# Four edits to the opening of a fused attention and double-MLP kernel: an early table load, two vectors on another queue, an earlier second pair, and square roots on another engine

## The chip, the cores and the metric

The kernel runs on one core of a Trainium2 chip. Its time is the device time of one execution in microseconds, and a kernel is judged by the median of several executions. One of them was taken with the hardware profiler; its trace and page are what is read below.

## The reference

`q`, `k` and `v` are [4, 12, 448, 64] in f32 (four batches, twelve heads, 448 rows, 64 columns). Everything that is computed:

```python
q_n = q / sqrt(mean(q*q, -1) + 1e-6) * g_q          # and k_n alike with g_k
attn = softmax(q_n @ k_n.T / 8)                      # per head
x = (attn @ v) laid out as [1792, 768]
h = x @ moe_w_in;   g = h * sigmoid(1.702 * h);   y = g @ moe_w_out       # 768 -> 2048 -> 768
h2 = y @ moe2_w_in; g2 = max(h2,0) + alpha*min(h2,0);  out = g2 @ moe2_w_out
```

Weights are f32 in memory. The two vectors g_q and g_k have 64 numbers each.

## The kernel before, in words

**Tiling and stages.** The twelve heads of a batch are handled as six pairs, so there are 24 pairs P (four batches b of six). A pair's q and k lie in one tile `qk` [128, 2, 7, 64], and its v in a second tile. `load_qk(P)` (L378 to L381) issues four transfers: the main rows of k and of q (192 KB each) and the remaining rows of k and of q (32 KB each). `load_v(P)` (L394 to L397) issues three. For the first batch both go to the queue of the sync engine SP, which issues them one after the other.

**The first batch** runs in f32. `normalize(P)` squares the pair on ScalarE in two halves (L421), sums each half on VectorE (L423) and computes the reciprocal roots of the 14 sums of every partition by a seed and three Newton steps (L424 to L434, 14 instructions on 128x14 elements; for a call with two pairs, 128x28), before the change always on GpSimd. `prep_pair(P)` multiplies q and k by the roots into `qn` (VectorE, L458), transposes `qn` on TensorE (L465, L467) and copies the result to SBUF on ScalarE (L468), k with the scale `g_col`, which holds the product of the gains. It then takes the maximum of v on VectorE (L470). The scores of the pair follow (L516, maximum L530, exponential L550).

**The gains.** `gains()` loads g_q and g_k, spread over the 128 partitions, multiplies them on VectorE (L284) and forms from them the scaled vector `gs` (L293), the constant `c_s` and, by a transposition on TensorE, the column `g_col` (L297).

**Weights beside it.** While the first pairs run, `weights(...)` streams the first layer's input weights through a ring of five raw buffers (transfers of 512 KB, L223, on SP's queue), turns each into f32 words (ScalarE L148, VectorE L164 and L165), takes row maxima (L245) and splits them into two f16 parts (L179, L180). The output weights follow. Then come the other three batches in f16 parts beside the first layer's products (L758, L798, L821), and at last the second layer (L927, L1090).

**The order of the work.** The program is written as generators that are advanced by hand (`first_pairs`, `attention`, `weights`), but the order in which an engine's instructions are issued is set by a planner, which moves ready work ahead of what is written before it, by priorities and a model of the times. On each engine's queue, and on SP's and GpSimd's transfer queues, work then runs in that fixed order. The opening is written in L1182 to L1191: identity and ones, `load_qk(0)`, `gains()`, `load_v(0)`, `load_qk(1)`, `load_v(1)`, then the first weight transfers, `normalize(0)`, `prep_pair(0)`, the loads of pair 2 and so on, and `normalize(1)`.

Of the kernel before, what the change touches and what calls it, by code (L numbers as in the profile page):

```python
# [9 lines left out]
F32 = mybir.dt.float32  # L10
# [47 lines left out]
def attention_moe_kernel(  # L58
# [220 lines left out]
    def gains():  # L279
        gq = small.tile([128, D], F32, tag="gq", name="gq", bufs=1)  # L280
        gk = small.tile([128, D], F32, tag="gk", name="gk", bufs=1)
        nc.sync.dma_start(out=gq, in_=g_q.partition_broadcast(128))
        nc.sync.dma_start(out=gk, in_=g_k.partition_broadcast(128))
        nc.vector.tensor_tensor(out=gq, in0=gq, in1=gk, op=ALU.mult)  # L284
        gm = small.tile([128, 1], F32, tag="gm", name="gm", bufs=1)
        gi = small.tile([128, 1], F32, tag="gi", name="gi", bufs=1)
        nc.vector.tensor_reduce(out=gm, in_=gq, op=ALU.max, axis=AX, apply_absolute_value=True)
        pow2floor(c_s, gm)
        scaled_reciprocal(gi, c_s, 0.5)
        nc.vector.memset(gs[64:128, 3], 1.0)  # L290
        for c in range(4):
            ps = slice(0, 64 if c == 3 else 128)
            nc.vector.tensor_scalar(out=gs[ps, c], in0=gq[ps], scalar1=gi[ps], scalar2=None, op0=ALU.mult)  # L293
        nc.vector.tensor_scalar(out=c_s, in0=c_s, scalar1=2.0 ** -22, scalar2=None, op0=ALU.mult)
        gt = ps_m.tile([128, 128], F32, tag="m", name="gt")
        nc.tensor.transpose(out=gt, in_=gs[:, 0:2].rearrange("p c d -> p (c d)"), identity=identf)
        nc.scalar.activation(out=g_col, in_=gt[:, 0:1], func=AF.Copy, scale=c_s)  # L297
# [111 lines left out]
    def normalize(*Ps):  # L409

        Ps = [P for P in Ps if P < B * NP]
        if not Ps:
            return
        n = NT2
        w = 2 * n * len(Ps)
        ss = small.tile([128, 4 * NT2], F32, tag="ss", name="ss")[:, 0:w]
        for t, P in enumerate(Ps):
            flat = raws[P].rearrange("p h c d -> p (h c) d")
            for i in range(2):
                sq = att_p.tile([128, n, D], F32, tag="sq", name="sq", bufs=SQB)  # L420
                nc.scalar.activation(out=sq, in_=flat[:, i * n:(i + 1) * n], func=AF.Square, scale=2.0 ** -13)  # L421
                o = (2 * t + i) * n
                nc.vector.tensor_reduce(out=ss[:, o:o + n], in_=sq, op=ALU.add, axis=AX)  # L423
        nc.gpsimd.tensor_scalar(out=ss, in0=ss, scalar1=1e-6 * 2.0 ** -20, scalar2=None, op0=ALU.add)  # L424
        rs = small.tile([128, 4 * NT2], F32, tag="rs", name="rs")[:, 0:w]
        tn = small.tile([128, 4 * NT2], F32, tag="tn", name="tn")[:, 0:w]
        nc.gpsimd.tensor_scalar(
            out=rs.bitcast(I32), in0=ss.bitcast(I32), scalar1=-0.5, scalar2=RSQRT_SEED, op0=ALU.mult, op1=ALU.add
        )
        for _ in range(3):  # L430
            nc.gpsimd.tensor_tensor(out=tn, in0=rs, in1=rs, op=ALU.mult)
            nc.gpsimd.tensor_tensor(out=tn, in0=tn, in1=ss, op=ALU.mult)
            nc.gpsimd.tensor_scalar(out=tn, in0=tn, scalar1=-0.5, scalar2=1.5, op0=ALU.mult, op1=ALU.add)
            rooted[Ps[0]] = nc.gpsimd.tensor_tensor(out=rs, in0=tn, in1=rs, op=ALU.mult)  # L434
        for t, P in enumerate(Ps):
            eng = side(P)
            ks = raws[P][:, :, 0:4]
            flat = raws[P].rearrange("p h c d -> p (h c) d")
            root = rs[:, 2 * n * t:2 * n * (t + 1)]
            if P < NP:  # L440
                roots[P] = root
                continue
            eng.tensor_tensor(out=ks, in0=ks, in1=gs.unsqueeze(1).to_broadcast([128, 2, 4, D]), op=ALU.mult)
            eng.tensor_tensor(out=flat, in0=flat, in1=root.unsqueeze(2).to_broadcast([128, 2 * n, D]), op=ALU.mult)
# [737 lines left out]
    if True:  # L1182
        make_identity(nc, ident)
        nc.vector.memset(ones, 1.0)
        nc.vector.tensor_copy(out=identf, in_=ident)
        load_qk(0)
        gains()
        load_v(0)
        load_qk(1)
        load_v(1)  # L1190
        g0 = big.tile([128, KF, 2, S], F16, tag="g", name="g0")  # L1191
        stage = g0.rearrange("p m e t -> p (m e t)").bitcast(F32)
        parts = stage[:, 0:R1I * 1024].bitcast(I32).rearrange("p (i n t) -> p i n t", i=R1I, t=2)
        raw1o = g0.rearrange("p m e t -> p m (e t)").bitcast(I32)[:, KF - 4 * R1O:, FIRST:].rearrange("p m (n t) -> p m n t", t=2)

        def num1i(j):
            if j == KD - 1:
                return stage[:, 5120:5120 + FF]
            return held.bitcast(F32)[:, (j - 3) * FF:(j - 2) * FF]

        def num1o(j):
            if j == KF - 2:
                return att_p.tile([128, 2 * NT2 * D], F32, tag="ph", name="num1o", bufs=PHB)[:, 0:DM]
            return raw_p.tile([128, 2 * NT2 * D], F32, tag="qk", name="num1o", bufs=QKB)[:, 0:DM]

        w1i_steps = weights(
            moe_w_in, "w1i", lambda: w1i, later_rows(w1i, 3, num1i), lambda t: parts[:, t % R1I], 4, R1I, 2.0 ** -14, scales,
            G1I
        )
        w1o_steps = weights(  # L1210
            moe_w_out, "w1o", lambda: w1o, later_rows(w1o, 2, num1o), lambda t: raw1o[:, 4 * (t % R1O):4 * (t % R1O) + 4], 2,
            R1O, 2.0 ** -25, scales, G1O
        )
        next(w1i_steps)
        normalize(0)
        for _ in prep_pair(0):
            pass
        for P in range(2, 1 + QKB):
            load_qk(P)
        load_v(2)  # L1220
        normalize(1)
        early = measure(1, B - 1, 4)
        for i, _ in enumerate(first_pairs()):
            if i >= 6:
                for _ in range(1):
                    next(early, None)
            for _ in range(W_RATE):
                next(w1i_steps, None)
        for _ in w1i_steps:
            pass  # L1230
        v_scales(0, v0)
        first_x()
        moe1_scales(0)
        for P in range(NP, NP + 2):
            load_qk(P)
            load_v(P)
        n1o = 0
        steps = attention([4 * P + r for P in range(NP) for r in range(2, 4)])
        for i, _ in enumerate(steps):
            pairs = max(0, (i - LAG + 1) // 2)  # L1240
            rows = KF - 2 if pairs >= 4 else (HOLD + pairs * HELD) // (2 * DM) - 2
            while n1o < min(1 + 2 * rows + 3 * (rows // 2), (i + 1) * W1O_RATE, 57):
                next(w1o_steps)
                n1o += 1
            if i >= M_AT and i - M_AT < KF:
                first_in(slice(0, FIRST), i - M_AT, g0)
            for _ in range(2):
                next(early, None)
        while n1o < 57:
            next(w1o_steps)  # L1250
            n1o += 1
        for m in range(len(range(2 * NP + LAG)) - M_AT, KF):
            first_in(slice(0, FIRST), m, g0)
        with tc.issue_after(loads["w1o"][W1O_HOLD].ins):
            normalize(NP, NP + 1)
            for _ in prep_pair(NP):
                pass
            load_qk(NP + 2)
            load_qk(NP + 3)
            load_v(NP + 2)  # L1260
        att_steps = other_batches()
        done = 4 * NP
        late = late_weights(ctx, att)
        for b in range(B):
            last = min(NU, 4 * NP * (b + 2)) + LAG2
            first = done
            got = None
            for i, _ in enumerate(moe1(b) if b else first_moe1(g0)):
                lead = 0 if b else B1_AT
                want = first + (last - first) * min(1.0, max(0.0, i + 1 - lead) / (PACE[b] * TICKS - lead))  # L1270
                while done < min(want, NU + LAG2):
                    next(att_steps)
                    done += 1
                if b == B - 1:
                    for _ in range(1 if i < 2 * KF else 2):
                        if got is None or i >= 2 * KF:
                            got = next(late, None)
        second_layer(late)
# [30 lines left out]
```

## Time and profile before

| what | value |
|---|---|
| time, median of 3 runs | 1150.96 us (1147.56 to 1157.47) |
| time of the profiled execution | 1150.36 us |
| its span, first to last instruction | 1148.6 us |
| TensorE (PE) busy | 1069.4 us, 93% of the span |
| VectorE (DVE) busy | 802.1 us, 70% |
| ScalarE (ACT) busy | 693.2 us, 60% |
| GpSimd (POOL) busy | 179.4 us, 16% |
| mean granted TensorE clock | 0.977 of full |
| moved by DMA | 158.19 MB, mean 138 GB/s |

The span is 1.8 us shorter than the execution's own time; what lies around it is not in the trace. Busy shares are averages over stages that differ: TensorE's 93% comes from the later stages, and the opening, where the diff is, looks different. Views by stretch and by order of time are therefore needed beside the table. "PEld" is TensorE's weight load, "SPq" the sync engine's queue of transfers.

### The profile page before, as it was taken

The numbers are of one execution on the slowest core, as the hardware profiler recorded it, in microseconds if no ns is written. First come the engines' busy times: TensorE is split into PE (matmuls) and PEld (weight loads), VectorE is DVE, ScalarE is ACT, GpSimd is POOL, SyncE is SP. The second block draws the span as 40 slices with busy tenths as digits, with TensorE's granted clock in tenths as the row PEclk, the third lists the DMA queues.
The fourth block names the chain that finished last, engine by engine and source line by source line (L and its number), as shares of the span: only waits on it lengthen the run. The fifth ranks groups of instructions, "written<-read, shape, count | busy, mean of one in ns | idle before, by whom it ended". The sixth has DMA issues, their size and how long they took to land.

```text
span 1148.6 us, 18408 instructions
## 1 busy us (share of the span) xinstructions
PE 1069.4 (93%) x6753; PEld 585.0 (51%) x6753; DVE 802.1 (70%) x1397; ACT 693.2 (60%) x1452; POOL 179.4 (16%) x364
## 2 busy tenths in 40 slices
PE   4776889898989999999999999999999999999998
PEld 2343457744444445555455455444444477666664
DVE  5979798887879885577534865599976224959341
ACT  4778686888879876688633562356456425756120
POOL 2701003676433342100000000000000000000000
PEclk9978899899999999999999999999999999999999
DMA  7974743478888756455446501765351423363111
GB/s 227 258 178 132 182 129 109 97 158 184 183 191 167 160 130 151 109 121 118 78 124 229 203 1 64 249 215 194 136 171 59 138 70 113 106 184 101 33 31 28
DMA packets 235562, 158.19 MB, mean 138 GB/s; under 512 B 167888, under 2 KB 214736, under 8 KB 235472
## 3 DMA queue, kind: packets, MB, share of 16 engines
q1 hardware_dynamic: 229200, 141.34, 44.6%
q0 software_dynamic: 6272, 15.67, 5.3%
q8 instruction: 53, 0.87, 0.3%
q14 instruction: 37, 0.30, 0.1%
HBM read 92.35 MB, written 25.69 MB: 103 GB/s over the span
## 4 chain that ended last, share of the span: by engine, by line
PE 56%; DVE 16%; DMA 11%; issue 7%; ACT 6%; POOL 4%; SPq 1%; DVEq 0%; POOLq 0%; ACTq 0%
PE op L1090 17%; PE yp L821 15%; PE h L927 9%; PE hp L798 7%; PE xp L648 3%; PE sp L525 2%; DMA t<-hl 2%; PE hp L758 2%; DMA g<-in_moe_w_in_dram 2%; DVE nm L530 1%; DMA g<-in_moe_w_out_dram 1%; DVE g L141 1%; ACT pr L550 1%; DMA qk<-in_q_dram 1%; DMA yr<-y_dram 1%
## 5 line engine op out<-in xcount | busy, mean ns | idle before, releaser
L821 PE MATMUL yp<-g,w1o 128*128 128x448 f16 x1152 | 226.9, 354 | 1.5 <-DVE g L767 0.9
L927 PE MATMUL h<-x,w2i 128*128 128x512 f16 (+1 forms) x1152 | 219.3, 352 | 4.3 <-DVE pos L933 2.8
L798 PE MATMUL hp<-x,w1i 128*128 128x448 f16 x864 | 170.3, 353 | 1.6 <-DVE t L807 1.6
L927 PEld LDWEIGHTS <-w2i 128*128 128x128 f16 x1152 | 112.6, 98 | 109.6 <-issue 5.1
L821 PEld LDWEIGHTS <-w1o 128*128 128x128 f16 x1152 | 109.5, 98 | 110.8 <-issue 12.0
L798 PEld LDWEIGHTS <-w1i 128*128 128x128 f16 x864 | 81.9, 98 | 83.5 <-issue 9.6
L620 DVE SCALAR_TENSOR_TENSOR ph<-pr,sm,ph 128x448 f16<-128x448 f32 x126 | 85.2, 707 | 25.4 <-ACT ph L593 25.4
L530 DVE TENSOR_REDUCE nm<-sp 128x2 f32<-128x896 f32 x96 | 92.5, 964 | 10.3 <-PE sp L525 7.6
L932 ACT ACTIVATE pos<-h,sign 128x512 f32<-128x512 f32 (+1 forms) x64 | 40.1, 628 | 89.7 <-PE h L927 83.3
L550 ACT ACTIVATE pr<-sp,nm,c_s 128x448 f32<-128x448 f32 x126 | 89.9, 717 | 2.4 <-DVE ph L620 1.1
L1090 PEld LDWEIGHTS <-even 128*128 128x128 f16 x672 | 65.7, 98 | 43.5
L933 DVE SCALAR_TENSOR_TENSOR pos<-h,slope,pos 128x512 f32<-128x512 f32 (+1 forms) x64 | 43.4, 680 | 59.9 <-ACT pos L932 59.7
L593 ACT ACTIVATE ph<-pr,sm 128x448 f16<-128x448 f32 x126 | 77.6, 659 | 10.7 <-DVE sm L590 10.6
L758 PE MATMUL hp<-x,w1i 128*128 128x256 f16 (+1 forms) x576 | 66.1, 276 | 9.2 <-DVE g L767 5.2
L1090 PEld LDWEIGHTS <-odd 128*128 128x128 f16 x504 | 49.3, 98 | 32.6
L758 PEld LDWEIGHTS <-w1i 128*128 128x128 f16 x576 | 55.2, 104 | 20.2 <-issue 14.8
L1090 PE MATMUL op<-w2lo,even 128*128 128x384 f16 x384 | 63.5, 326 | 0.0
L648 PE MATMUL xp<-pt,vs 128*64 128x256 f16 (+1 forms) x792 | 49.8, 267 | 7.5 <-DMA pt<-ph 6.2
L525 PE MATMUL sp<-t 64*128 64x448 f16 (+1 forms) x432 | 54.0, 357 | 0.6 <-DMA t<-hl 0.5
L648 PEld LDWEIGHTS <-vs 128*64 128x64 f16 x792 | 37.9, 112 | 27.6 <-issue 17.2
L532 ACT ACTIVATE nm<-nm,c_s 128x2 f32<-128x2 f32 x72 | 20.9, 290 | 48.5 <-DVE nm L530 48.1
L1090 PE MATMUL op<-w2hi,even 128*128 128x384 f16 x288 | 47.5, 326 | 0.0
(243 smaller groups left out, 1659.7 us busy)
## 6 DMA issues: line engine op xcount, KB each, us to landing
g<-in_moe_w_in_dram SPq DMA_DIRECT2D x24, 512.0 KB, 6.1
g<-in_moe_w_out_dram SPq DMA_DIRECT2D x32, 384.0 KB, 4.0
w2raw<-in_moe_w_in_dram SPq DMA_DIRECT2D x24, 512.0 KB, 5.7
w2raw<-in_moe_w_out_dram SPq DMA_DIRECT2D x16, 768.0 KB, 6.4
g_dram<-pos SPq DMA_DIRECT2D x48, 256.0 KB, 2.0
gp<-g_dram SPq DMA_DIRECT2D x8, 1024.0 KB, 6.8
odd<-g_dram SPq DMA_DIRECT2D x6, 1024.0 KB, 5.5
y_dram<-y SPq DMA_DIRECT2D x24, 224.0 KB, 2.5
```

What stands on the lines that cost most here:

```text
L525: nc.tensor.matmul(out=sp[:, j, 0:S] if n == 2 else sp[ds, 0, 0:S], lhsT=qt[ds] if n == 2 else qt[ds, 64:128], rhs=kt[ds, 0:S], start=(i = ...
L530: nc.vector.tensor_reduce(out=nm[:, 0:n], in_=sp[:, 0:n, 0:S], op=ALU.max, axis=AX, negate=True)
L550: last = nc.scalar.activation(out=pr[i], in_=sp[:, i, 0:S], func=AF.Exp, bias=nm[:, i:i + 1], scale=c_s if u >= 4 * NP else 1.0, accum_out ...
L593: nc.scalar.activation(out=ph[:, i, 0:S], in_=pr[i], func=AF.Copy, scale=sm[:, i:i + 1])
L620: nc.vector.scalar_tensor_tensor(out=ph[:, i, S:2 * S], in0=pr[i], scalar=sm[:, i:i + 1], in1=ph[:, i, 0:S], op0=ALU.mult, op1=ALU.subtract)
L648: nc.tensor.matmul(out=xp[64 * j:64 * j + 64, t:t + n], lhsT=vs[ks, j, c], rhs=pt[ks, 7 * j + kc, 0:n] if b else pt[ks, kc, o:o + n], star ...
L758: nc.tensor.matmul(out=ps, lhsT=w1i[:, kk, e, m * 128:(m + 1) * 128], rhs=xs[0, kk][:, f, cols], start=(i == 0), stop=(i == 3 * KD - 1))
L798: nc.tensor.matmul(out=ps, lhsT=w1i[:, kk, e, m * 128:(m + 1) * 128], rhs=x[:, f], start=(n == 0), stop=(n == 3 * KD - 1))
L821: nc.tensor.matmul(out=ps, lhsT=w1o[:, m, e, j * 128:(j + 1) * 128], rhs=g[:, m, f], start=(n == 0), stop=(n == 3 * KF - 1))
L927: nc.tensor.matmul(out=ps, lhsT=w2i[:, kk, e, m * 128:(m + 1) * 128], rhs=x2[kk][:, f], start=(c == 0), stop=(c == 3 * KD - 1))
L933: nc.vector.scalar_tensor_tensor(out=pos, in0=ps, scalar=slope[:, m:m + 1], in1=pos, op0=ALU.mult, op1=ALU.max)
L1090: nc.tensor.matmul(out=ps, lhsT=ops[:, o, m, f], rhs=rhs[:, e], start=(c == 0), stop=(c == 3 * KH - 1))
```

## The change

Four edits, all in the opening:

1. A small activation (`first`, 128x1, function Square, read from `ones`) is added ahead of everything else on ScalarE.
2. The transfers of g_q and g_k are issued by GpSimd instead of SP.
3. `load_qk(1)` is issued right after `load_qk(0)`, ahead of `load_v(0)`.
4. The 14 root instructions of pair 0 go to VectorE; those of all other pairs stay on GpSimd.

```diff
     def gains():
...
-        nc.sync.dma_start(out=gq, in_=g_q.partition_broadcast(128))
-        nc.sync.dma_start(out=gk, in_=g_k.partition_broadcast(128))
+        nc.gpsimd.dma_start(out=gq, in_=g_q.partition_broadcast(128))
+        nc.gpsimd.dma_start(out=gk, in_=g_k.partition_broadcast(128))
...
     def normalize(*Ps):
...
-        nc.gpsimd.tensor_scalar(out=ss, in0=ss, scalar1=1e-6 * 2.0 ** -20, scalar2=None, op0=ALU.add)
+        eng = nc.vector if Ps[0] < 1 else nc.gpsimd
+        eng.tensor_scalar(out=ss, in0=ss, scalar1=1e-6 * 2.0 ** -20, scalar2=None, op0=ALU.add)
...
-        nc.gpsimd.tensor_scalar(
+        eng.tensor_scalar(
             out=rs.bitcast(I32), in0=ss.bitcast(I32), scalar1=-0.5, scalar2=RSQRT_SEED, op0=ALU.mult, op1=ALU.add
         )
         for _ in range(3):
-            nc.gpsimd.tensor_tensor(out=tn, in0=rs, in1=rs, op=ALU.mult)
-            nc.gpsimd.tensor_tensor(out=tn, in0=tn, in1=ss, op=ALU.mult)
-            nc.gpsimd.tensor_scalar(out=tn, in0=tn, scalar1=-0.5, scalar2=1.5, op0=ALU.mult, op1=ALU.add)
-            rooted[Ps[0]] = nc.gpsimd.tensor_tensor(out=rs, in0=tn, in1=rs, op=ALU.mult)
+            eng.tensor_tensor(out=tn, in0=rs, in1=rs, op=ALU.mult)
+            eng.tensor_tensor(out=tn, in0=tn, in1=ss, op=ALU.mult)
+            eng.tensor_scalar(out=tn, in0=tn, scalar1=-0.5, scalar2=1.5, op0=ALU.mult, op1=ALU.add)
+            rooted[Ps[0]] = eng.tensor_tensor(out=rs, in0=tn, in1=rs, op=ALU.mult)
...
         make_identity(nc, ident)
         nc.vector.memset(ones, 1.0)
+        first = small.tile([128, 1], F32, tag="first", name="first", bufs=1)
+        nc.scalar.activation(out=first, in_=ones[:, 0:1], func=AF.Square)
         nc.vector.tensor_copy(out=identf, in_=ident)
         load_qk(0)
+        load_qk(1)
         gains()
         load_v(0)
-        load_qk(1)
         load_v(1)
```

## Rows read from the trace of the kernel before

**Rows 1.** Busy time by stretch; columns: engines, granted clock, DMA share, GB/s.
```profile
0.00:20.00 20.00, 5.10 (x15) 2.72 (x17) 8.97 (x25) 6.93 (x12) 7.44 (x33) 1.00 0.67 214
20.00:40.00 20.00, 11.87 (x37) 5.23 (x34) 19.50 (x32) 14.74 (x30) 8.88 (x24) 1.00 0.95 282
40.00:60.00 20.00, 15.86 (x102) 9.04 (x102) 18.36 (x37) 12.95 (x30) 14.61 (x37) 1.00 0.86 248
60.00:80.00 20.00, 17.44 (x80) 9.16 (x80) 16.55 (x32) 16.24 (x38) 1.68 (x3) 0.70 0.80 171
...
140.00:160.00 20.00, 18.54 (x132) 11.17 (x129) 15.69 (x39) 14.17 (x33) 0.00 (x0) 0.92 0.54 156
...
240.00:260.00 20.00, 20.00 (x160) 10.28 (x155) 16.93 (x29) 17.59 (x42) 15.86 (x25) 1.00 0.80 172
...
500.00:600.00 100.00, 100.00 (x685) 50.76 (x683) 59.58 (x101) 66.83 (x155) 3.84 (x6) 1.00 0.47 107
```

**Rows 2.** Order of time, the first pair's path from its load to `qn` on all engines.
```profile
2.55 0.61 SPq L381 DMA_DIRECT2D qk<-in_q_dram  x1
...
4.79 1.28 ACT L421 ACT_TABLE_LOAD   x1 [4.79 <-DMA qk<-in_q_dram]
...
6.09 1.04 ACT L421 ACTIVATE sq<-qk 128x448 f32<-128x448 f32 x2
...
8.60 0.23 DVE L284 TENSOR_TENSOR gq<-gq,gk 128x64 f32<-128x64 f32 x1 [1.28 <-DMA gk<-in_g_k_dram]
8.74 0.61 DVE L423 TENSOR_REDUCE ss<-sq 128x7 f32<-128x448 f32 x1
...
9.45 0.26 POOL L424 TENSOR_SCALAR ss<-ss 128x14 f32<-128x14 f32 x1 [8.15 <-DVE ss L423]
...
13.34 0.22 POOL L434 TENSOR_TENSOR rs<-tn,rs 128x14 f32<-128x14 f32 x1
13.59 1.09 DVE L458 TENSOR_TENSOR qn<-qk,rs 128x896 f32<-128x896 f32 x1 [0.39 <-POOL rs L434]
...
15.30 0.26 POOL L424 TENSOR_SCALAR ss<-ss 128x14 f32<-128x14 f32 x1 [1.74 <-DVE ss L423]
...
20.47 1.09 DVE L458 TENSOR_TENSOR qn<-qk,rs 128x896 f32<-128x896 f32 x1 [1.00 <-POOL rs L434]
```

**Rows 3.** Order of time, SP's queue from g_q to the first weights.
```profile
3.21 0.59 SPq L282 DMA_DIRECT2D gq<-in_g_q_dram  x1
...
4.32 0.43 SPq L394 DMA_DIRECT2D w1o<-in_v_dram  x1
...
6.10 0.59 SPq L378 DMA_DIRECT2D qk<-in_k_dram  x1
...
8.55 0.59 SPq L394 DMA_DIRECT2D w1o<-in_v_dram  x1
...
10.59 2.57 SPq L223 DMA_DIRECT2D g<-in_moe_w_in_dram  x5
```

**Rows 4.** Chain that ended last; start, length, what.
```profile
3.84 4.65 DMA gk<-in_g_k_dram
...
25.36 6.55 DMA qk<-in_q_dram
```

**Rows 5.** Order of time, short VectorE instructions of the gains, and v's maximum.
```profile
9.52 0.15 DVE L105 TENSOR_SCALAR c_s<-gm 128x1 f32<-128x1 f32 x1
9.70 0.15 DVE L106 TENSOR_SCALAR c_s<-c_s 128x1 int32<-128x1 int32 x1
...
10.00 0.69 DVE L470 TENSOR_REDUCE v<-w1o 128x1 f32<-128x512 f32 x1
```

**Rows 6.** Order of time, two transfers issued by GpSimd.
```profile
48.86 1.34 POOL L312 DMA_DIRECT2D vst<-in_v_dram  x2
```

**Rows 7.** Transfers by line; count, KB each, median us from issue to landing.
```profile
vr<-in_v_dram POOLq DMA_DIRECT2D x32, 32.0 KB, 3.1
```

**Rows 8.** Order of time: a load of the second layer, issued in the opening.
```profile
44.51 0.42 SPq L857 DMA_DIRECT2D slope<-in_moe_alpha_dram  x1
```

## The prediction

> **What bounds the kernel now.** I first read the busy time by stretch [rows 1], because the whole-span shares of 93% for TensorE and 70% for VectorE hide the order of the limits. From about 240 us on TensorE is busy nearly all the time; the stretches from 240 to 260 us (20.00 of 20) and from 500 to 600 us (100.00 of 100) stand for it. What starts there earlier ends earlier, so a microsecond saved in front reaches the end if it reaches 240 us. In front of that no engine is full all the time. In the first 20 us VectorE works 8.97 us and stands for 11.0, while the transfers are at a share of 0.67. From 20 to 40 us VectorE is busy 19.50 of 20 and the transfers are at 0.95: both are nearly full there, and the share of the transfers falls only after 40 us.
>
> Second, I read the opening in order of time [rows 2]. Pair 0's last load is issued at 2.55 us and releases ScalarE at 4.79, but ScalarE then loads its table of functions for 1.28 us, and the squares start at 6.09. The second sum's input is there at 7.13 (6.09 + 1.04), yet VectorE's queue holds the product of the gains in front of it, which waits 1.28 us for g_k; so the sum starts at 8.74. GpSimd's 14 instructions run from 9.45 to 13.56, and `qn` starts at 13.59. For pair 1 GpSimd starts at 15.30 and `qn` at 20.47, after VectorE stood still for 1.00 us.
>
> Third, SP's queue [rows 3]: g_q at 3.21, the first v at 4.32, pair 1's q and k at 6.10, the second v at 8.55, the first weights at 10.59. The chain that ended last [rows 4] runs through g_k (4.65 us from issue to landing), and at 25.36 through a load of q of 6.55 us. So the opening is a chain of latencies, and the 30 us behind it are bound by transfers as much as by VectorE.
>
> **The change part by part.** *Early table load.* The load needs nothing but ScalarE, which is idle before 4.79. Released by `ones`, ready about 1 us into the span, it and the small activation are over before pair 0 lands, and the squares start at 4.8 instead of 6.09: 1.3 us less on the path [rows 2]. The cover is the load of q and k. The Trainium skill, "ScalarE: Activation LUTs", section "What ACT_TABLE_LOAD costs", adds a drain of 1.38 us and so puts a switch at 2.66 us. This trace shows the 1283 ns but no drain behind them: the load ends at 6.07 and the squares begin at 6.09. By the page the term would be 2.7 us; I keep 1.3.
>
> *Gains on GpSimd's queue.* Two transfers leave SP: 4.32 − 3.21 = 1.11 us, by which everything after `load_v(1)`, the weights first, is issued earlier [rows 3]. GpSimd spends 1.34 us on two issues [rows 6] and is otherwise idle there until the sums come. It can issue them from about 1.3 us; they land 3.1 us later by the nearest row of its queue [rows 7], or at most 4.65 by the g_k of SP [rows 4]: at 5.1 to 7.3 us instead of 8.49. If the product of the gains still stands between the two sums, it costs VectorE at best no wait, and at worst, with squares ready at 5.86, about a microsecond; I take none. So the second sum ends near 6.7 instead of 9.36, of which 1.3 us is the table and 1.3 the gains.
>
> *Pair 0's roots on VectorE.* GpSimd takes 4.1 us (9.45 to 13.56). Dependent short instructions on VectorE follow each other every 0.18 us (9.52, 9.70 [rows 5]), on one element; the upper end is the product of the gains with 64 elements, 0.23 [rows 2], some 0.26 with the gap. So 14 of them cost 2.5 to 3.6 us; 14 elements are nearest the short rows, and I take 2.5. That is 1.6 us less in latency and 2.5 us more work for VectorE, which stands idle for 11.0 us of these 20 [rows 1]; without that cover it would cost its 2.5 us in full. If the gains' eleven instructions (2.2 us by rows like these) come ahead of the roots on VectorE's queue, `qn` is that much later. Together pair 0's `qn` starts at 9.2 to 11.4 instead of 13.59: 2.2 to 4.4 us earlier.
>
> *Pair 1 ahead of v.* Its four transfers take 2.45 us on SP (6.10 to 8.55) and move up by 2.89: 1.11 for the gains and 1.78 for the three transfers of v that they pass. GpSimd, free of pair 0, can start pair 1's roots near 10 instead of 15.30. The first v is issued 2.45 − 1.11 = 1.34 us later; the second v and the weights still gain 1.11. VectorE reads the first v at 10.00 [rows 5]; that cover is thin, which is a rival below.
>
> **The sum.** The latency chain gets 2.2 to 4.4 us shorter, the transfers start 1.11 us earlier. Between 15 and 40 us both limit, so I expect the front to move by something between 1.1 and 4.4 and take 2.5: 1150.36 − 2.5 = 1147.9 us, **1148**. The profiled execution lies 0.6 us under the median of the runs shown, well inside their spread of 10 us, so I make no correction.
>
> **Rivals.** *Only the transfers count.* With their share at 0.95 [rows 1] and a 6.55 us load on the chain [rows 4], an earlier `qn` only waits longer for weights; the result is 1.1 us or nothing, 1149.3 to 1150.4. For it: the full transfers. Against: the share is not 1.00, and the weights' ring is refilled only when VectorE has consumed it. The same time follows if the edits are inert, for instance if the planner places the table load or the gains so that nothing starts earlier. The Trainium skill, "DMA: Bandwidth & Descriptors", section "Issuing engines are not separate DMA queues", says that issuing from several engines saves only issue time; the trace agrees in that SP's issues, not the bytes of g_q and g_k (64 KB), are what stands ahead of the weights.
>
> *VectorE waits for the first v.* Now issued at 5.66 to 7.4, it lands by 11.5 at the latest (an issue at 6.8 plus 4.65 [rows 4]). If the maximum of v stays ahead of the roots in VectorE's order, they begin at 11.5 + 0.69 = 12.2 and `qn` at 14.7, 1.1 us later than before: 1151.5. It decides if v's maximum is placed ahead of pair 0's `qn`, as it is before.
>
> *Slower: TensorE's granted clock.* From 60 to 80 us the mean granted clock is 0.70, a mixture of 1.2 and 2.4 GHz, after TensorE had worked 15.86 of the 20 us before; from 140 to 160 it is 0.92 [rows 1]. A new order of the front shifts when TensorE works and stands. At the lower level throughout, the work of the first slice needs 17.44 × 0.70 / 0.5 = 24.4 us, 4.4 more than there are; that of the second 18.54 × 0.92 / 0.5 = 34.1, 14.1 more. It decides where the granted clock falls below 0.61 in the first slice (17.44 × 0.70 / 20) or 0.85 in the second. That gives 1155 to 1164. For it: the planner orders the whole program, as the second layer's slope, loaded at 44.51 us, shows [rows 8], so the order after 60 us need not be the old one. Against: an earlier opening is no reason for a lower clock.
>
> *Faster by more.* The same mechanism with the other sign: at the full level the work of the first slice takes 12.2 us, 5.2 less, and over 60 to 160 us there are some such slices; with the earlier opening, 1133 to 1145. TensorE is only one of the limits there (VectorE has 16.55 of 20), so the lower end is remote.
>
> **How the numbers follow.** Forecast (1146.0 to 1149.3) 0.50; only the transfers or inert 0.20; waiting for v 0.08; slower by clock or order 0.11; faster by it 0.11. The first three hold 0.78 between 1146 and 1151.5. The sizes of the last two are the least certain, and the runs before spread over 10 us, so the range reaches some way into each, to where about 0.04 is left out on either side: 1140 to 1158. About 1% (11.5 us) is what a measurement of this kernel can tell from no change: below 1139.4 lies only the far part of the faster case, 0.07; above 1162.5 the far part of the slower one, 0.05; 0.88 between.
>
> **What would show it.** In the changed trace: the table load near 1 us and squares at 4.8; the gains issued by GpSimd and landed before 7.3; no wait of VectorE between pair 0's sums; 14 short VectorE instructions in 2.5 to 3.6 us; `qn` at 9.2 to 11.4 and pair 1's near 15; the first weights issued at 9.5. The first scores' maximum and the weights' row maxima then show how much of it is left at 25 and at 60 us, and the start of the full stretch after 240 us what reaches the end. I am wrong if `qn` is early and the full stretch is not, or if the granted clock between 60 and 180 us differs.

## The result: 0.66% slower, and the profile after

The changed kernel takes 1158.47 us (median of 13 runs, 1153.26 to 1164.38), the kernel before on the same chip 1149.72 us (13 runs, 1146.41 to 1157.47): a ratio of 1.0066, 95% interval [1.0044, 1.0087]. Forecast were 1148.0 us and a range of 1140 to 1158. So the sign was wrong and the time lies 0.47 us above the range; it is within 1% of before, as expected with 0.88. The profiled execution of the changed kernel took 1156.52 us with a span of 1154.8 us. Three executions below (the profiled ones of c0, 2372 us, and of m512, 2755 us, and one of e1, 1400 us) lasted far longer than all others and are left out of the ratios, and no row is read from the two profiles.

First, the opening, after, in order of time (start us, us, engine, line, operation; in brackets the idle time before it and its releaser). It answers to [rows 2, 3].

```profile
0.73 1.28 ACT L1187 ACT_TABLE_LOAD   x1 [0.73 <-PEq L1296]
...
1.28 0.70 POOL L282 DMA_DIRECT2D gq<-in_g_q_dram  x1 [0.36 <-issue]
...
2.54 0.62 SPq L381 DMA_DIRECT2D qk<-in_q_dram  x1
...
3.21 0.60 SPq L378 DMA_DIRECT2D qk<-in_k_dram  x1
...
5.84 0.60 SPq L394 DMA_DIRECT2D w1o<-in_v_dram  x1
...
6.98 0.22 DVE L284 TENSOR_TENSOR gq<-gq,gk 128x64 f32<-128x64 f32 x1 [3.79 <-DMA gk<-in_g_k_dram]
...
7.37 1.04 ACT L421 ACTIVATE sq<-qk 128x448 f32<-128x448 f32 x2 [5.15 <-DMA qk<-in_q_dram]
...
8.58 0.61 DVE L423 TENSOR_REDUCE ss<-sq 128x7 f32<-128x448 f32 x1
...
9.22 0.17 DVE L425 TENSOR_SCALAR ss<-ss 128x14 f32<-128x14 f32 x1
9.31 0.14 DVE L112 TENSOR_SCALAR gi<-c_s 128x1 f32<-128x1 f32 x1
9.43 0.17 DVE L428 TENSOR_SCALAR rs<-ss 128x14 int32<-128x14 int32 x1
...
9.71 2.79 SPq L223 DMA_DIRECT2D g<-in_moe_w_in_dram  x5
...
10.47 1.13 DVE L423 TENSOR_REDUCE ss<-sq 128x7 f32<-128x448 f32 x2
...
11.59 0.67 DVE L471 TENSOR_REDUCE v<-w1o 128x1 f32<-128x512 f32 x1
...
14.59 1.09 DVE L459 TENSOR_TENSOR qn<-qk,rs 128x896 f32<-128x896 f32 x1
...
18.17 1.09 DVE L459 TENSOR_TENSOR qn<-qk,rs 128x896 f32<-128x896 f32 x1 [0.34 <-PE qt L468]
```

The table is loaded at 0.73 us, as intended, but pair 0's last transfer, issued at 2.54 as before, now releases the squares at 7.37 us, where it released ScalarE at 4.79. The 14 roots begin at 9.22 and end at 14.55, with other work between them. So pair 0's `qn` starts 1.0 us later than before, pair 1's 2.3 us earlier (18.17 against 20.47).

That is not where the 7 us are. Matching each instruction with its like in the two traces, the medians of the lag by stretch of 30 us are within about 3 us of before up to 330 us, but for a stall of up to 9 us between 60 and 90 that is made up by 120. From there the lag grows to 7 us at 420 us and stays until the end. So the loss is made where three batches of attention run beside the first layer. There, the DMA queues of the kernel before between 200 and 430 us (packets, MB, share of the 16 engines; then transfers with their count and median us to landing). "q1" is the hardware queue that carries SP's transfers; `ph` are the softmax's values and `hl` a pair's q and k, both in f16 parts, which transfers transpose into `pt` and `t1` (shown as `t`):

```profile
q1 hardware_dynamic: 95363, 25.46, 53.9%
...
pt<-ph SPq DMA_TRANSPOSE x53, 3.7
...
t<-hl SPq DMA_TRANSPOSE x13, 3.9
```

The same of the changed kernel:

```profile
q1 hardware_dynamic: 95136, 25.21, 64.9%
...
pt<-ph SPq DMA_TRANSPOSE x52, 4.5
...
t<-hl SPq DMA_TRANSPOSE x13, 5.2
```

The packets and bytes are the same within 1%, but their time has grown from 53.9 to 64.9% of sixteen engines, and a transpose lands 0.8 to 1.3 us later. What TensorE waited for in that stretch, before (us in total, times, longest; `xp` is the product with v, `hp` the first layer's):

```profile
PE xp L648 <- DMA pt<-ph: 6.2, 3, 3.2
PE hp L758 <- DVE g L767: 5.0, 2, 3.1
PE hp L758 <- DVE last_t L767: 1.4, 1, 1.4
```

And after:

```profile
PE xp L649 <- DMA pt<-ph: 10.1, 10, 2.4
PE hp L759 <- DVE g L768: 6.1, 6, 1.9
PE hp L759 <- DVE last_t L768: 3.8, 1, 3.8
PE xp L649 <- DVE ph L621: 2.8, 1, 2.8
```

These rows alone are 10.2 us longer (22.8 against 12.6), more than the loss. Only the first names a transfer; the other three name VectorE. One profile is no proof of either: f2 below, whose time is that of before, has 10.4 us in the row of `pt`, in a profiled execution of 1154.20 us (its median is 1149.69). The clock isn't the cause: its mean in the same stretch is 0.97 before and 0.99 after (the third number from the right). Over whole executions, a0 below and the kernel before on the same chip were granted the same mean, 0.977, and a0 is still slower by 0.58%.

```profile
200.00:430.00 230.00, 213.82 (x1621) 115.59 (x1621) 193.27 (x336) 195.49 (x473) 116.26 (x210) 0.97 0.72 158
200.00:430.00 230.00, 205.26 (x1579) 111.06 (x1580) 187.26 (x319) 189.77 (x464) 114.61 (x201) 0.99 0.84 155
```

The slice in which the prediction feared a lower clock does have one, after (0.92 before [rows 1]):

```profile
140.00:160.00 20.00, 15.35 (x107) 9.74 (x105) 14.11 (x37) 12.50 (x32) 0.00 (x0) 0.83 0.50 145
```

### The profile page after: what moved, and what is told of

Its sections match the earlier page's. It is cut to its first block, busy times and chain, and to the rows that moved or that the text cites. A ratio compares the mean times of both kernels' runs of the same rounds, so it can differ in the third digit from the quotient of the medians.

```text
span 1154.8 us, 18409 instructions
## 1 busy us (share of the span) xinstructions
PE 1062.6 (92%) x6753; PEld 581.3 (50%) x6753; DVE 802.9 (70%) x1411; ACT 691.4 (60%) x1453; POOL 179.1 (16%) x352
## 4 chain that ended last, share of the span: by engine, by line
PE 57%; DMA 13%; DVE 13%; issue 6%; ACT 6%; POOL 3%; SPq 2%; ACTq 0%; DVEq 0%; POOLq 0%
PE op L1091 17%; PE yp L822 14%; PE hp L799 10%; PE h L928 9%; PE xp L649 3%; DMA t<-hl 2%; PE sp L526 2%; DMA g<-in_moe_w_out_dram 2%; DMA pt<-ph 2%; DMA qk<-in_q_dram 2%; ACT pr L551 1%; DMA yr<-y_dram 1%; DVE nm L531 1%; DVE w2num L165 1%; DMA g<-in_moe_w_in_dram 1%
## 5 line engine op out<-in xcount | busy, mean ns | idle before, releaser
L759 PE MATMUL hp<-x,w1i 128*128 128x256 f16 (+1 forms) x576 | 62.0, 266 | 12.7 <-DVE g L768 8.0
L649 PE MATMUL xp<-pt,vs 128*64 128x256 f16 (+1 forms) x792 | 50.1, 265 | 12.9 <-DMA pt<-ph 10.1
```

The lines of the kernel that those rows point to most:

```text
L649: nc.tensor.matmul(out=xp[64 * j:64 * j + 64, t:t + n], lhsT=vs[ks, j, c], rhs=pt[ks, 7 * j + kc, 0:n] if b else pt[ks, kc, o:o + n], star ...
L759: nc.tensor.matmul(out=ps, lhsT=w1i[:, kk, e, m * 128:(m + 1) * 128], rhs=xs[0, kk][:, f, cols], start=(i == 0), stop=(i == 3 * KD - 1))
```

## The experiments

Ratios are to the kernel before, run on the same chip, as on record; the quotient of the medians differs from them by up to 0.002 (y1: 1156.07 / 1149.82 = 1.0054, on record 1.0033). Two facts of the compiled programs made the experiments possible. The new 4-byte tile `first` takes 32 bytes per partition in front of the gains' tiles, so all tiles allocated behind it, those of the transposes among them, lie 32 bytes higher. And the planner's order changed far beyond the opening: some 310 of VectorE's 1397 shared instructions stand elsewhere, and so do some 230 of ScalarE's, 40 of SP's transfers and part of TensorE's work. Of the four edits made alone, the table load leaves the order as it was, while each of the other three changes it. "Old order" below means that behind the opening every engine follows the order of the kernel before. c0, c2, e1, n1, p2, q256 and q128 have it from the planner; the others are held to it (edges between consecutive instructions of an engine, from a list).

| kernel | tiles moved by | order | q1 share, 200 to 430 us | `pt` lands, us | ratio [interval] |
|---|---|---|---|---|---|
| before | 0 | old | 53.9% | 3.7 | 1 |
| c0, a comment only | 0 | old | - | - | 1.0017 [0.9991, 1.0042] |
| c2, one memset | 0 | old | 54.7% | 3.7 | 0.9992 [0.9975, 1.0010] |
| f2, gains alone | 0 | old | 55.4% | 3.7 | 1.0003 [0.9982, 1.0024] |
| y2, change, no tile | 0 | old | 53.9% | 3.7 | 0.9991 [0.9965, 1.0017] |
| y3, gains on SP, no tile | 0 | old | 54.3% | 3.7 | 0.9989 [0.9964, 1.0014] |
| m512 | -512 | old | - | - | 0.9984 [0.9957, 1.0011] |
| q256 | 256 | old | 55.4% | 3.8 | 1.0013 [0.9989, 1.0037] |
| q128 | 128 | old | 62.4% | 4.3 | 1.0040 [1.0014, 1.0067] |
| n1, idle tile | 32 | old | 61.6% | 4.2 | 1.0060 [1.0036, 1.0085] |
| e1, table alone | 32 | old | 63.4% | 4.5 | 1.0069 [1.0040, 1.0097] |
| p2, table alone | 64 | old | 60.3% | 4.3 | 1.0058 [1.0036, 1.0080] |
| x1, change | 32 | old | 63.1% | 4.2 | 1.0049 [1.0025, 1.0074] |
| x3, gains on SP | 32 | old | 63.2% | 4.3 | 1.0050 [1.0028, 1.0073] |
| p4, gains on SP | 64 | old | 63.8% | 4.2 | 1.0057 [1.0024, 1.0089] |
| x2, no edit | 0 | new | 55.6% | 3.9 | 1.0062 [1.0039, 1.0085] |
| y1, change, no tile | 0 | new | 56.5% | 3.8 | 1.0033 [1.0009, 1.0056] |
| a0, change again | 32 | new | 63.4% | 4.3 | 1.0058 [1.0021, 1.0095] |
| p3, change | 64 | new | 64.9% | 4.5 | 1.0063 [1.0037, 1.0090] |
| after, the change | 32 | new | 64.9% | 4.5 | 1.0066 [1.0044, 1.0087] |

**Order or opening?** x1 has all four edits and the old order; x2 no edit and the changed kernel's order behind the old opening; e1 the table load alone; x3 the table, the roots on VectorE and pair 1 early, with the gains left on SP and the old order. In x3 the list also lays out the opening by hand: pair 1's loads ahead of the first v, and the gains on VectorE behind pair 0's `qn`.

```diff
         attention_moe_kernel(tc, *args)
+        in_order(tc)     # x1, x3: the list of before; x2: that of the changed kernel (lists cut)
```
```diff
         nc.vector.memset(ones, 1.0)
+        first = small.tile([128, 1], F32, tag="first", name="first", bufs=1)
+        nc.scalar.activation(out=first, in_=ones[:, 0:1], func=AF.Square)     # all of e1
```

> All four edits, with the changed kernel's own opening up to pair 0's qn; behind it every engine issues in the order of the kernel before. Theory 'order' (the loss of 9 us is made by the planner's other order between 310 and 430 us, not by the opening): 1147 to 1152 us, ratio to before 0.998 to 1.002, and no loss between 310 and 430 us. Theory 'opening' (pair 0 lands 2.6 us later and qn starts 1 us later, and that delay is what grows): 1156 to 1160, ratio about 1.006, as the changed kernel.

> None of the four edits: the kernel before with its own opening up to pair 0's qn; behind it every engine issues in the order that the planner gave the changed kernel. Theory 'order': 1155 to 1160 us, ratio 1.005 to 1.009, with the loss between 310 and 430 us. Theory 'opening': 1147 to 1152, ratio about 1.000.

> Only the early table load; the planner leaves every other instruction in its old order. Theory of the prediction: squares start 1.3 us earlier, but the second sum still waits for g_k behind the product of the gains, so at most 0.2 us of it reaches qn; 1149 to 1151, ratio 0.999 to 1.001. If an earlier table load were worth its 1.3 us: 1148.5.

> Early table load and pair 0's roots on VectorE, the gains left on SP's queue; order of the kernel before behind the opening. In the opening the roots and qn stand directly behind pair 0's sums, the gains behind qn, and pair 1's q and k are issued after the gains and ahead of the first v. Prediction's theory (an earlier qn reaches the end): qn at 9.2 to 10 us, 3.5 to 4.4 us earlier, and 1146 to 1148.5, ratio 0.997 to 0.999. Rival (the transfers of the weights bound the opening): qn as early, but 1149 to 1151, ratio about 1.000.

All four are 0.5 to 0.7% slower, so neither theory alone holds: the old order doesn't rescue the edits, and the new order costs without them. e1 was the surprise: same order, table out of the way, and still 1.0069.

**The tile's place.** n1 adds an idle 4-byte tile to the kernel before; p2, p3 and p4 are e1, the change and x3 with the new tile padded to 64 bytes.

```diff
+        idle0 = small.tile([128, 1], F32, tag="idle0", name="idle0", bufs=1)      # n1
+        nc.gpsimd.memset(idle0, 0.0)
...
-        first = small.tile([128, 1], F32, tag="first", name="first", bufs=1)
+        first = small.tile([128, 16], F32, tag="first", name="first", bufs=1)[:, 0:1]   # p2, p3, p4
```

> The kernel before with one more tile of 4 bytes a partition (filled once by GpSimd in its idle first microsecond, read by nobody), in the place where the change puts its tile of the early activation; the order of all other instructions is the old one. The tile takes 32 bytes and moves every later SBUF tile by 32, so that the tiles of the transposing transfers no longer begin at a multiple of 64 bytes. Theory 'placement' (the loss comes from this shift, which slows the packets of the transposing transfers): 1155 to 1158 us, ratio 1.005 to 1.008, transfers' share from 200 to 430 us up from 54% to about 63% on SP's queue. Theory 'timing' (any disturbance of the opening costs this much): 1149 to 1151, ratio 1.000, for nothing is disturbed but a GpSimd that was idle.

> The early table load alone, as in e1, with its tile made 64 bytes wide, so that later tiles move by 64 bytes instead of 32. Theory 'placement': the 6.6 us of e1 are gone: 1148.5 to 1150.5, ratio 0.998 to 1.001. Theory 'timing': as e1, 1156, ratio 1.006.

> The changed kernel, every instruction in its place, with the tile 64 bytes wide. If placement made the whole loss: 1147 to 1151, ratio 0.998 to 1.001. If the planner's new order has a loss of its own, as x2 with 1.006 says: 1155 to 1158, ratio 1.005 to 1.007.

> x3 (clean opening, old order behind it) with the tile 64 bytes wide. Theory 'placement': 5 to 7 us less than x3, that is 1149 to 1151; if the earlier qn reaches the end besides, 1146 to 1149, ratio 0.997 to 0.999. Theory 'timing': as x3, 1156.

The idle tile costs as much as the whole change. Padding to 64 bytes doesn't help, against what p2, p3 and p4 expected of a cause that lies in the place. At this point everything but the kernel before itself was slow, and the comparison was suspect too.

**Controls.** c0 adds a comment; c2 a memset of a tile that exists, so no tile moves; f2 puts the gains alone on GpSimd's queue in the old order; a0 is the change once more.

```diff
-from contextlib import ExitStack
+from contextlib import ExitStack  # the kernel before
...
+        nc.gpsimd.memset(g_col, 0.0)     # c2, not in c0
```

> The kernel before with one comment added at the end of its first line: no instruction, address or place in an order differs. Seven kernels so far, with very different edits, all measured 1.005 to 1.007 of the kernel before. Theory A (the offset lies in the comparison: whatever is measured beside the kernel before comes out about 0.6 per cent longer): 1.004 to 1.007, about 1156 us, and the transposing transfers between 200 and 430 us show a share of over 60 per cent and land in 4.3 us or more. Theory B (any real alteration of the program loses 7 us in that stretch, because the kernel before is at a lucky spot): 0.998 to 1.002, about 1150 us, share near 54 per cent. Theory C (the change's own parts cost the time): also 0.998 to 1.002.

> The kernel before with one more GpSimd memset, of a tile that exists already and that a later memset fills again: no tile is added and no address moves, the order on every engine stays, POOL's first transfer issue starts some 0.1 us later. Theory A (comparison): 1.004 to 1.007. Theory B with addresses (the shift of the tiles by 32 or 64 bytes loses it): 0.998 to 1.002. Theory B with any instruction (the smallest shift of the opening's times loses it): 1.004 to 1.007 while the comment alone stays at 1.000.

> Only the two gain loads on GpSimd's queue, every other instruction in the order of the kernel before; no tile added, no address moved. In the opening: if the 64 packets of 2 KB from GpSimd's queue are what delays the first pair, its squares start at 7 us or later (4.79 before) and the first qn at 15 to 16 us (13.59 before), with the second pair still in its old place; if it is the second pair's early transfers that delay it, the squares stay at 4.8 to 5.3 us. In the time: A 1.004 to 1.007 like everything else; otherwise the opening's 2 us are absorbed by the first pair's slack and it measures 1.000 to 1.003.

> The changed kernel once more, beside the comment-only copy on the same chip. Theory A: both stand at 1.004 to 1.007, their quotient within 0.998 to 1.002, so that the four edits together move nothing. Theories B and C: this one 1.005 to 1.008 and the copy at 1.000.

The comparison is sound: c0, c2 and f2 stand at 1, the change again at 1.0058. f2 also shows in order of time what delays pair 0, since its pair 1 stays behind v:

```profile
1.29 0.70 POOL L282 DMA_DIRECT2D gq<-in_g_q_dram  x1 [0.36 <-issue]
...
7.10 1.28 ACT L421 ACT_TABLE_LOAD   x1 [7.10 <-DMA qk<-in_q_dram]
...
14.53 1.09 DVE L458 TENSOR_TENSOR qn<-qk,rs 128x896 f32<-128x896 f32 x1 [0.40 <-POOL rs L434]
```

Pair 0's load releases ScalarE at 7.10 us instead of 4.79, with the gains alone moved. Its DMA queues in the first 12 us show the gains' 64 packets (32 of 2 KB, 32 of 4 bytes):

```profile
q0 software_dynamic: 64, 0.07, 9.5%
```

That is 1.1 us of each of the sixteen engines (0.095 x 12), while pair 0's packets wait. Single packets in the trace show it: half of the 32, as many as there are engines, took 0.66 to 1.27 us each, and from 3.5 to 4.5 us only 36 of the queue's 256-byte packets began, against 263 in the trace of before. In the time it costs nothing that can be measured (1.0003).

**Settling it.** m512 moves the tiles by exactly 512 bytes, by letting the gains share a later tile; y1 is the change in its own order, y2 is x1 and y3 is x3, each without the new tile.

```diff
-        gq = small.tile([128, D], F32, tag="gq", name="gq", bufs=1)      # m512
-        gk = small.tile([128, D], F32, tag="gk", name="gk", bufs=1)
+        g2 = small.tile([128, 2 * D], F32, tag="row", name="row", bufs=1)
+        gq, gk = g2[:, 0:D], g2[:, D:2 * D]
...
-        first = small.tile([128, 1], F32, tag="first", name="first", bufs=1)   # y1, y2, y3
-        nc.scalar.activation(out=first, in_=ones[:, 0:1], func=AF.Square)
+        nc.scalar.activation(out=g_col, in_=ones[:, 0:1], func=AF.Square)
```

> The kernel before with its tiles behind the two gain tiles moved down by exactly 512 bytes (the gains share a 512-byte tile that is used later anyway); no instruction is added, the order is that of before. So far every kernel whose tiles moved by 32 or 64 bytes shows 60 to 65 per cent of the engines' time on the hardware queue between 200 and 430 us and 1.005 to 1.007 of the time, while the four with unmoved tiles show 54 to 56 per cent. In the kernel before, the tiles that the transposing transfers read and write lie at multiples of 512 bytes. Theory P (a multiple of 512, or of a smaller power of two above 64, is what matters): 54 to 56 per cent, transposes of ph land in 3.7 us, 0.998 to 1.002. Theory Q (any move loses it, the kernel before being at one lucky spot): 60 to 65 per cent, 4.2 to 4.5 us, 1.004 to 1.007.

> All four edits as in the change, in the changed kernel's own order, but the first function's result goes into an existing tile (g_col, which a later function of the same engine fills): no tile is added and none moves. If moved tiles are all of the loss: hardware queue at 54 to 56 per cent between 200 and 430 us, time 0.997 to 1.001. If the changed order costs by itself, as before's code in that order did (1.0062): queue at 54 to 56 per cent and still 1.003 to 1.007.

> All four edits without a new tile, and behind the opening the order of the kernel before. The only thing left is the opening: its first qn is some 1.0 us later, its second pair 2.3 us earlier. If tiles and order are the two causes: 54 to 56 per cent on the queue, 0.997 to 1.001. If the four edits themselves cost: 1.003 or more. The prediction's own sum for the opening would be 0.998.

> Table first, the first pair's roots on VectorE and the second pair early, with the gains left on SP's queue, no new tile and the order of before: the opening in which the first qn starts at 9.5 us instead of 13.59. If the 4 us of the opening reach the end: 0.996 to 0.997, about 1146 us. If they are swallowed by the first pair's slack before 130 us: 0.998 to 1.001. If tiles were not the cause of the same kernel's 1.005 with the tile: 1.003 to 1.006.

A move as such costs nothing that can be measured (m512), and without a move neither do the four edits in the old order (y2, 0.9991 against 1.0049 with the tile). The changed order costs by itself: y1, 1.0033, and x2, 1.0062. A mark of it is on TensorE's waits between 200 and 430 us, in y1:

```profile
PE xp L649 <- DMA pt<-ph: 10.6, 8, 2.4
PE hp L759 <- DVE g L768: 4.7, 3, 2.2
PE hp L759 <- DVE last_t L768: 3.8, 1, 3.8
PE sp L526 <- ACT pr L551: 3.1, 3, 2.2
PE xp L649 <- DVE ph L621: 2.7, 1, 2.7
```

In y2:

```profile
PE xp L649 <- DMA pt<-ph: 8.4, 6, 3.4
PE hp L759 <- DVE g L768: 5.6, 3, 3.0
PE sp L526 <- ACT pr L551: 1.9, 2, 1.5
```

The waits for `ph` and `last_t`, both made by VectorE, are in y1 as in the changed kernel, and not in y2. Over all profiles, `last_t` is waited for 3.8 us in each of the five kernels with the new order and at most 1.4 us in the old; `ph` 2.6 to 3.1 us in four of the five, but not in x2. A different place of these two in VectorE's order fits that; it wasn't tried alone, and the other engines' order changed with it, so what in the new order costs the time stays open.

The row of `pt` tells the tile's part, but in the old order only: 6.2 to 10.4 us in the six profiles with tiles unmoved or moved by 256 bytes, 10.8 to 15.6 in the seven with a move of 32, 64 or 128. In the new order it is 10.2 and 10.6 us without a move and 9.6 to 10.1 with one.

**How coarse?** The idle tile of n1 made 256 and 128 bytes wide.

```diff
+        idle0 = small.tile([128, 64], F32, tag="idle0", name="idle0", bufs=1)[:, 0:1]   # q128: 32
+        nc.gpsimd.memset(idle0, 0.0)
```

> The idle tile of the kernel with an identical order made 256 bytes wide (one GpSimd memset of its first 4 bytes): every later tile moves by 256 bytes, off the multiples of 512. If only multiples of 512 bytes will do: 60 to 65 per cent on the hardware queue between 200 and 430 us, 1.004 to 1.007, as with 32 and 64 bytes. If multiples of 256 or 128 do: 54 to 56 per cent, 0.997 to 1.002, as with a move by 512.

> The same with the idle tile 128 bytes wide. If multiples of 128 bytes do, 54 to 56 per cent and 0.997 to 1.002; if 256 or 512 are needed, 60 to 65 per cent and 1.004 to 1.007.

The DMA queues of q256 between 200 and 430 us:

```profile
q1 hardware_dynamic: 95136, 25.21, 55.4%
...
pt<-ph SPq DMA_TRANSPOSE x53, 3.8
```

And of q128, with the same packets and bytes:

```profile
q1 hardware_dynamic: 95136, 25.21, 62.4%
...
pt<-ph SPq DMA_TRANSPOSE x52, 4.3
```

256 bytes keep the old speed, 128 don't. By address, the transposes' tiles (`hl`, `ph`, `pt` and the tile behind `hl`) begin at multiples of 256 bytes in every kernel of the table with 53 to 57%, and off them in every one with 60 to 65%. ("The tile behind `hl`" is `t1`.) All later tiles moved together, but the packets in the two traces tell the transfers apart. Of the 95136, 5536 have 4, 384 or 1792 bytes (by their counts, those of 384 and 1792 are `vs` and the first layer's stored results) and took 147 us in both, summed over the engines. The 89600 of 256 bytes, which leaves them to the transposes, took 1892 us in q256 and 2150 in q128: the median packet takes 18 ns in both, but 7546 take 30 to 60 ns in q128 and 363 in q256 (7509 in n1, 502 before). So it is the transposes that get longer; whether the tile that they read or the one that they write has to be aligned is not separated.

The multiple has a page: the Trainium skill, "DMA: Bandwidth & Descriptors", section "How a descriptor splits into AXI transactions", says that a transaction starts at a multiple of 256 bytes, so that a piece that doesn't begin there fetches bytes that it doesn't use. The runs agree on the multiple (256 and 512 keep the time, 32, 64 and 128 lose it); the extra bytes themselves show in no trace here, whose packets count the same, and of which one in twelve gets longer (7546 of 89600) and not every one.

## Why the prediction was wrong, point by point

*Early table load: the step that failed.* The load itself did as said, and its cover held. But the step took the small activation as free, hidden behind pair 0's load, and its 4-byte destination moved the tiles of transfers that run 200 us later. At equal order that is 1.0049 against 0.9991 (x1, y2), nearly 7 us, and no rival covered it. The idle tile n1 shows that neither the load nor the activation does it.

*The rival "Slower: TensorE's granted clock"*, in the chances "slower by clock or order", had 0.11, and its time (1155 to 1164) holds the result. It brought in the planner's new order only as something that could shift the clock, and the sum took the work behind the opening to keep its order. The order was real: alone it costs 0.33% (y1) to 0.62% (x2). The clock, from which the time was worked out, was not, so that the time fits is luck: after, the slice from 140 to 160 us was granted less than before, 0.83 against 0.92 [rows 1], yet no lag was left at 200 us. The two causes seem to add to less than their sum: tile and order together gave 1.0066 and 1.0058, about what either gives, though with y1's 0.33% for the order the sum (0.33 + 0.58) is not clear of the intervals. The waits for `pt` fit that, which the tile lengthens in the old order and not in the new; why was not tested.

*Gains on GpSimd's queue* is a second step that failed, though it cost no measurable time at the end. The forecast for their landing was right (by 6.98 us, within 5.1 to 7.3), and SP issued the weights 0.88 us earlier. But the prediction put their 64 KB down as nothing to the transfers beside them. f2 shows pair 0 landing 2.3 us later for them, and that is why the squares start at 7.37 and not at 4.8. The rule that it quoted (the Trainium skill, "DMA: Bandwidth & Descriptors", section "Issuing engines are not separate DMA queues") also says that transfers from different engines run on the same 16 DMA engines and interleave; f2's 2.3 us agree with that half, which the prediction didn't draw on.

*Roots on VectorE* were priced at 2.5 to 3.6 us, and 2.5 was taken. With the gains on SP and VectorE's opening laid out by hand, y3 shows it, in order of time:

```profile
4.72 1.04 ACT L421 ACTIVATE sq<-qk 128x448 f32<-128x448 f32 x2 [2.50 <-DMA qk<-in_q_dram]
5.33 1.14 DVE L423 TENSOR_REDUCE ss<-sq 128x7 f32<-128x448 f32 x2 [3.77 <-ACT sq L421]
6.51 0.17 DVE L425 TENSOR_SCALAR ss<-ss 128x14 f32<-128x14 f32 x1
6.72 0.17 DVE L428 TENSOR_SCALAR rs<-ss 128x14 int32<-128x14 int32 x1
...
9.43 1.09 DVE L459 TENSOR_TENSOR qn<-qk,rs 128x896 f32<-128x896 f32 x1
```

From 6.51 to 9.43 they take 2.9 us, 0.21 each, and `qn` starts at 9.43, within the forecast 9.2 to 11.4. In the changed kernel the late landing brought pair 0's roots together with the gains, pair 1's sums and two maxima of v, and they took 5.3 us. The prediction had named the gains' eleven instructions as a risk, and v's maximum as a rival that leaves `qn` 1.1 us later than before; `qn` came 1.0 us late, with v's maxima among the roots as one part of it. Its bound of 11.4 counts the gains' 2.2 us, but not its own upper price of the roots (3.6), with which it would be 12.5.

*Pair 1 ahead of v* went the way that was forecast, by less: its roots start on GpSimd at 11.69 us (forecast near 10, before 15.30) and its `qn` at 18.17 (forecast near 15, before 20.47).

*The sum.* The term of 2.5 us for the opening is not borne out at the end, not even in its direction. y3's opening is 4.2 us ahead at the first `qn`, 2 to 3 us from 30 to 260 us, 1.4 us at 420 us, and the whole measures 0.9989 [0.9964, 1.0014]: -1.3 us, between -4.1 and +1.6. y2, with the gains in the way, measures 0.9991. Neither can be told from no change. Both are faster than the change as made. So that a microsecond gained by 240 us reaches the end is not shown here. The chances don't fit together either: about 0.04 was left out below 1140 and above 1158 us, yet 0.07 given to what lies below 1139.4 and 0.05 to what lies above 1162.5.

## What to carry to other kernels

A new tile is an edit to the address of every tile behind it: reuse an existing one (y2) or pad it to 256 bytes (q256), or, untried here, allocate it last, and run an idle tile of its size as a control before explaining anything else. Where a planner orders the program, an edit's own worth can only be read with the rest of the order held, so test edit and order apart. A small load moved to another queue still takes its packets' time on shared engines, so look at what lands beside it, not only at who issues it (f2).

## What the runs showed of the hardware

The time of the transfers on the queue of the transposes depends on where their tiles begin in SBUF: with 95136 packets and 25.21 MB in each, the queue took 55.4% of the engines' time at a move of 256 bytes, and 62.4, 60.3 and 61.6% at 128, 64 and 32. What gets longer are the transposes' 256-byte packets: about 7500 of 89600 took 30 to 60 ns at a move of 128 or 32, 363 at a move of 256, while the median stayed at 18 ns. Two vectors of 64 numbers, spread over 128 partitions in 64 packets, took 9.5% (f2) and 11.1% (after) of sixteen engines for 12 us, 16 of f2's packets 0.66 us or more each, and another queue's landing was put off by 2.3 us (f2) to 2.6 (after). And short dependent instructions on VectorE (128x14) follow each other every 0.21 us (6.51, 6.72 in y3), but instructions of two independent chains every 0.09 to 0.12 us (9.22, 9.31, 9.43, after): an instruction of one chain starts in the gap of the other.
